# A sparse-attention and feed-forward kernel: sampled indices packed and loaded once, gathers and values' results for eight heads of a tile, and a schedule built from other durations

## The chip, the cores and the metric

The kernel runs on one core of a Trainium2 chip. The number that counts is the time of one execution in microseconds (us) on that core. A core has a matrix engine (TensorE, PE in the rows), three engines for elementwise work (VectorE or DVE, ScalarE or ACT, GpSimd or POOL), a queue engine that here only issues DMAs (SyncE or SP), and 16 DMA engines that serve the DMAs of all queues. Each engine runs its own instructions in order; an instruction that waits holds up all that stand behind it on that engine.

## The reference

Block-sparse attention over 4 batches, 8 heads, 768 positions and 64 channels, then a feed-forward layer. Each query block of 32 positions sees its neighbours, the first and last block, and three blocks that `sampled_blocks` names; the first and last query block see everything. The feed-forward weights are stored as float64.

```python
scores = scale * np.matmul(q, k.transpose(0, 1, 3, 2))
mask = np.abs(blk_i - blk_j) <= window
mask = mask | (blk_i == 0) | (blk_j == 0) | (blk_i == n_blocks - 1) | (blk_j == n_blocks - 1)
for qb in range(n_blocks):
    for kb in sampled_blocks[qb]:
        mask[qb * block:(qb + 1) * block, kb * block:(kb + 1) * block] = True
scores = np.where(mask, scores, -1000000000.0)
attn = np.exp(scores - np.max(scores, axis=-1, keepdims=True))
attn = attn / (np.sum(attn, axis=-1, keepdims=True) + 1e-09)
x = np.matmul(attn, v)            # (B, H, S, D), then to rows of H * D
h = x @ w_in                      # (3072, 512) @ (512, 2048)
g = np.maximum(h, 0.0) + alpha * np.minimum(h, 0.0)
out = g @ w_out                   # (3072, 2048) @ (2048, 512)
```

## The kernel before

Every number is split into a high and a low half in float16, and a product is the sum of high times high, high times low and low times high.

Attention is cut into 48 **units** (batch `b`, query tile `t` of 128 positions, half `c` of four heads). A tile is shifted by 32 positions, so that five of the six tiles of a batch hold only sparse blocks (40 sparse units), and the sixth holds the first and last block (8 dense units). A sparse unit goes through these steps:

- `emit_kr` (POOL): gathers the sampled blocks of the transposed keys into `kr`, 12 copies whose source address is a register. `picks` loads the 12 registers (L526) for each unit.
- `emit_vr` (SP): gathers the sampled blocks of the split values from a scratch tensor in DRAM into `vr`, 12 DMAs with an address from a register (L538), and again 12 register loads ahead of them on SP.
- `emit_s`, `emit_r` (PE): scores into the four PSUM banks `sp`.
- softmax: `emit_bias` (DVE, L635), `emit_exp` (ACT, L642), the two halves `ph` (`emit_p_hi`, `emit_p_lo`), and `emit_p_t` (SP, L683), a DMA transpose of `ph` to `pt`.
- `emit_r`, `emit_av` (PE, L555): values into one PSUM bank `av` per unit, `[hi part | low part]` beside each other, so that one matmul of 128 columns and one of 64 do a product.
- `evict`: the sum of the two parts (`emit_x_sum`, DVE, L688), the softmax division (L693), the split (L697, L701), and a DMA transpose on SP (L708) into `x`.

The feed-forward layer (`moe`) works on 12 chunks of 256 rows. A chunk has eight pairs of an up group `emit_up` (24 matmuls, L1050, into the one PSUM bank `h`) and a down group `emit_down` (12 matmuls, L1085). Between them stand `emit_act` on DVE (L1059, L1060), `emit_gh` on ACT and `emit_gl` on POOL (L1068). A chunk needs `x` of two tiles.

At the start, 16 pieces each of `w_in` (`wi`) and `w_out` (`wo`) are loaded, turned from float64 into float32 on DVE (L909, L916, L921), squared and scaled. The scale of `wo` is one for the whole matrix: a sum over all 16 pieces (`emit_o_tot`) and a matmul that spreads it (`emit_o_bc`, through L482).

What sets the order: each step is entered in a `Plan` with a priority, a cost in us for each engine that may do it, and buffers that it takes and frees. `Plan.run` plays the steps through and hands out an order, which is then fixed on every engine. The costs written there are a gather of values on SP at 1.5, a gather of keys on POOL at 5.0, a transpose on SP at 2.4, and loads on ACT alone at 0.06.

## Time and profile before

| | us |
|---|---|
| median of 3 runs | 1015.63 (1012.66 to 1015.92) |
| the profiled execution | 1017.7 |
| its span, first to last instruction | 1015.6 |
| PE busy in the span | 761.2 |
| mean granted clock of TensorE | 0.865 |

A row of the waits names the engine and the line that waited, what it waited for, the total in us, the number of waits and the longest. A row of the windows gives, for a stretch, its length and then the busy time of PE, PE's weight loads (PEld), DVE, ACT and POOL, the granted clock of TensorE, the share of the 16 DMA engines that was busy, and GB/s. "SPq" is SP issuing. A row of the timeline is a run of instructions with its start, its length, and in brackets the idle time ahead of it.

### The profile page before, as it was taken

To read this page: it belongs to the slowest core of one execution; us is meant where nothing else is said; L and a number is where in the kernel's file an instruction comes from. 1 tells how busy PE (TensorE), PEld (TensorE's weight loads), DVE (VectorE), ACT (ScalarE), POOL (GpSimd) and SP (SyncE) were. 2 spreads that over 40 slices of the span, in tenths; PEclk is the share of its full clock that TensorE was granted. 3 is DMA by queue.
4 is the path that set the end of the run, shared out by engine and by line. 5 is a ranking of instruction groups with operands and counts; after the bars stand their busy time and mean duration, and the time that the engine had idled before them with its cause. 6 is when DMAs were issued, how large, how long until landed. Compare 5 with 4: busy or idle time off the path is not lost.

```text
span 1015.6 us, 22541 instructions
## 1 busy us (share of the span) xinstructions
PE 761.2 (75%) x7931; PEld 510.4 (50%) x7931; DVE 638.9 (63%) x1535; ACT 374.7 (37%) x854; POOL 330.0 (32%) x676
## 2 busy tenths in 40 slices
...
GB/s 219 211 284 169 207 167 108 158 161 149 165 146 128 149 91 76 154 157 174 170 134 146 111 89 148 145 147 166 161 120 164 108 82 133 76 99 140 53 26 21
DMA packets 378737, 139.94 MB, mean 138 GB/s; under 512 B 338161, under 2 KB 367873, under 8 KB 378625
## 3 DMA queue, kind: packets, MB, share of 16 engines
...
## 4 chain that ended last, share of the span: by engine, by line
PE 32%; issue 13%; DMA 9%; DVE 8%; SPq 5%; POOL 3%; ACT 2%; POOLq 1%; ACTq 1%; DVEq 0%
PE h L1050 13%; PE o L1085 12%; PE sp L555 4%; DMA pt<-ph 3%; PE av L555 3%; SPq L538 2%; POOL gl L1068 2%; SPq L526 2%; DVE g L1059 2%; DVE ph L364 1%; POOL kr L550 1%; DMA qs<-qt 1%; DVE g L1060 1%; DMA x<-xn 1%; DMA qt<-qn 1%
## 5 line engine op out<-in xcount | busy, mean ns | idle before, releaser
L1050 PE MATMUL h<-x,wi 128*128 128x256 f16 x2304 | 286.0, 284 | 21.7 <-DVE g L1060 14.8
L1050 PEld LDWEIGHTS <-wi 128*128 128x128 f16 x2304 | 231.2, 102 | 67.4 <-issue 23.6
L1085 PE MATMUL o<-wo,gh 128*128 128x512 f16 x768 | 243.2, 400 | 1.5 <-ACT gh L1064 1.5
L1068 POOL TENSOR_TENSOR gl<-g,gh 128x512 f16<-128x512 f32 x96 | 117.6, 1226 | 371.7 <-ACT gh L1064 349.8
L550 POOL COPY kr<-kt 128x128 f16 x480 | 153.4, 374 | 179.2 <-PE sp L555 128.2
L1085 PE MATMUL o<-wo,gl 128*128 128x512 f16 x384 | 153.8, 401 | 25.4 <-POOL gl L1068 25.4
L1059 DVE TENSOR_SCALAR g<-h,am 128x256 f32<-128x256 f32 x192 | 83.8, 478 | 139.2 <-PE h L1050 132.8
L1064 ACT CAST gh<-g 128x512 f16<-128x512 f32 x96 | 59.1, 615 | 293.1 <-DVE g L1060 267.9
L642 ACT ACTIVATE e<-e,nm 128x352 f32<-128x352 f32 x160 | 92.6, 579 | 79.3 <-DVE nm L635 47.0
L364 DVE SCALAR_TENSOR_TENSOR ph<-e,ph 128x704 f16<-128x704 f32 (+1 forms) x106 | 102.7, 976 | 25.2 <-ACT ph L356 25.0
L1085 PEld LDWEIGHTS <-gh 128*128 128x128 f16 x768 | 73.8, 102 | 82.5 <-issue 16.2
L555 PEld LDWEIGHTS <-pt 96*32 96x32 f16 (+1 forms) x2304 | 74.0, 106 | 77.3 <-DMA pt<-ph 58.6
L555 PE MATMUL sp<-kt,qt 128*128 128x192 f16 (+2 forms) x384 | 67.1, 257 | 55.7 <-DVE nm L635 40.1
L635 DVE CUSTOM_DVE_ANT_0 e<-sp,bias,cs 128x352 f32<-128x352 f32 x160 | 86.8, 575 | 20.8 <-PE sp L555 20.7
L555 PE MATMUL sp<-kt,qs 128*128 128x192 f16 (+2 forms) x384 | 67.7, 259 | 16.3 <-DMA qs<-qt 16.3
L1085 PEld LDWEIGHTS <-gl 128*128 128x128 f16 x384 | 39.3, 102 | 80.3 <-POOL gl L1068 31.6
L555 PEld LDWEIGHTS <-qt 128*32 128x32 f16 (+1 forms) x1024 | 46.7, 104 | 62.7 <-issue 34.8
L1060 DVE SCALAR_TENSOR_TENSOR g<-h,gsc,g 128x512 f32<-128x512 f32 x96 | 72.1, 751 | 3.4
L555 PE MATMUL av<-vr,pt 96*32 96x128 f16 (+1 forms) x1280 | 28.9, 233 | 50.3 <-DMA pt<-ph 49.4
L555 PEld LDWEIGHTS <-qs 128*32 128x32 f16 (+1 forms) x1024 | 45.3, 104 | 38.8 <-issue 19.7
L356 ACT ACTIVATE ph<-e 128x704 f16<-128x704 f32 (+1 forms) x62 | 49.7, 804 | 32.6 <-DMA pt<-ph 17.9
L688 DVE TENSOR_REDUCE xf<-av 128x256 f32<-128x512 f32 x48 | 32.8, 684 | 44.3 <-PE av L555 44.3
...
## 6 DMA issues: line engine op xcount, KB each, us to landing
...
```

What stands on the lines that cost most here:

```text
L356: nc.scalar.activation(dst, src, AF.Copy, scale=scale)
L364: nc.vector.scalar_tensor_tensor(dst, src, scale, hi, ALU.mult, ALU.subtract)
L550: nc.gpsimd.tensor_copy(kr[:, :, g, r * BLK : (r + 1) * BLK], kt[:, :, bass.ds(i * BLK, BLK)])
L555: nc.tensor.matmul(dst, lhs, rhs, start=start, stop=False, skip_group_check=True)
L635: nc.vector.tensor_tensor_reduce(T["e", u, h // 2][:, h % 2, :CS], T["sp", u, h][:, :CS], bias[:, t], scale=T["cs", b, t][:, c : c + 1], s ...
L642: nc.scalar.activation(e, e, AF.Exp, bias=T["nm", u, h], scale=-1.0, accum_out=su_of(u)[:, h : h + 1])
L1050: nc.tensor.matmul(ph[:, i, :], win(w, f, ct), x[:, ct // 2, l, ct % 2, :], start=(m == 0), stop=(m == len(terms) - 1))
L1059: nc.vector.tensor_scalar(g[:, i, :], ph[:, i, :], 0.0, am1[:, f : f + 1], ALU.min, ALU.mult)
L1060: nc.vector.scalar_tensor_tensor(g, ph, gsc[:, j : j + 1], g, ALU.mult, ALU.add)
L1064: nc.scalar.copy(T["gh", c, j], T["g", c, j])
L1068: nc.gpsimd.tensor_tensor(T["gl", c, j], T["g", c, j], T["gh", c, j], ALU.subtract)
L1085: nc.tensor.matmul(T["o", c][t], g[:, i, t * P : (t + 1) * P], wout(w, f), start=(f == 0 and m == 0), stop=(f == NF - 1 and m == 2),)
```

## The change

Five things are different.

- **Indices.** Two block numbers are packed into one word (`spack`, DVE), and POOL and SP each load 30 registers once, at the program's start. A gather takes its 12 numbers from them by a mask or a shift. The loads of 12 registers, 40 on SP and 40 on POOL, are gone.
- **Gathers of values.** `emit_vr` runs once for a tile and fetches all eight heads: 20 times 12 DMAs of 64 KB instead of 40 times 12 of 32 KB.
- **Values' results.** The eight heads of a tile share one PSUM bank. A product takes three matmuls of 64 columns that add into the same place, where it took one of 128 and one of 64; the sum over the two parts falls away, and division, split and transpose run once for a tile (24 times instead of 48). The scale of `v` is found for each half of the heads, and the division evens the two out (`fac`).
- **Start.** Keys of the first batch and the first query tile are transposed by PE (with copies on ACT or DVE) and no longer by DMA. Loads may be issued by SP as well as ACT. In batches after the first, the small matmuls for the scales of `k` and `v` go to the bank `h`, which the up groups use, instead of `av`.
- **Schedule.** Costs and priorities in the plan are others, and steps of one kind are chained in order. `P_PE = 0` leaves all transposes of `ph` with SP.

```diff
-MOE_LAG = 7.669
+MOE_LAG = 14.222
 MOE_BOOST = 7.439
-V_WI = -2.266
+V_WI = 2.0
 W_WI = 0.799
-V_WO = -2.974
+V_WO = 4.06
...
-PL_V = -35.527
-P_V = 3.0
-LD = 5
+PL_W = 30.0
...
+P_V = -3.693
+P_K0, P_K1 = -10.0, 3.746
+KB0, KB1, KL0, KL1 = -5.461, -8.133, -22.947, -14.0
+VB0, VB1, VL0, VL1 = -4.453, -6.0, -20.0, -9.725
+GK, GV = (6, 3), (5, 3)
+P_Q, PL_Q = 10.31, 12.632
+A_UP = 0.511
+X_UP = 0.863
+LD = 3
 LAG = 0
 RAWP = ["x", "vr"]
-BUFS = {"vf": 4, "qf": 1, "qn": 1, "qt": 2, "qs": 2, "ph": 4, "e": 3, "pt": 5, "xf": 1, "xn": 2, "x": 3,
-        "g": 3, "sid": 1, "kt": 3, "v2": 3, "vb": 2, "vr": 2, "kr": 2, "gh": 3, "gl": 3}
+KVP = ["vf", "x"]
+BUFS = {"vf": 3, "qf": 1, "qn": 1, "qt": 2, "qs": 2, "ph": 4, "e": 3, "pt": 4, "xf": 1, "xn": 1, "x": 3,
+        "g": 3, "sid": 1, "kt": 3, "v2": 5, "vb": 2, "vr": 2, "kr": 2, "gh": 3, "gl": 3}
+K_PE = 2
...
     sidx = cpool.tile([1, NBLK, NR], I32, name="sidx")
+    spack = cpool.tile([1, TS * NG4 * NR // 2], I32, name="spack")
...
+    pairs = sidx.rearrange("p a r -> p (a r)")[:, NR : NR + TS * NG4 * NR].rearrange("p (n w) -> p n w", w=2)
+    nc.vector.scalar_tensor_tensor(
+        spack, pairs[:, :, 1], 16, pairs[:, :, 0], ALU.logical_shift_left, ALU.bitwise_or
+    )
+    idx = {}
+    for name, eng in (("g", nc.gpsimd), ("s", nc.sync)):
+        regs = [eng.alloc_register(name=f"{name}{i}") for i in range(TS * NG4 * NR // 2)]
+        eng.load(regs, spack)
+        idx[eng] = []
+        for r in regs:
+            v = eng.snap(r)
+            idx[eng] += [
+                nc.s_assert_within(x, 0, NBLK - 1, skip_runtime_bounds_check_because="clamped to this range before the load")
+                for x in (v & 0xFFFF, v >> 16)
+            ]
...
-    LQ = {"ACT": 0.06}
-    MAX4 = {"DVE": (0.55, 0), "ACT": 0.85, "POOL": 1.05}
-    LOW4 = {"DVE": (0.94, 0), "POOL": (1.05, 1.65)}
-    PHI = {"DVE": (0.55, 0), "ACT": 0.85}
+    LQ = {"ACT": 0.45, "SP": 0.35}
+    LQ3 = {"ACT": 1.3, "SP": 1.0}
...
+    def emit_k_pe(b, c, h):
+        if ("kt", b, c) not in T:
+            T["kt", b, c] = wt("kt", [P, HQ, S], F16)
+        nat = kn_view(b, c, h // 2)
+        t = T["kp", b, c, h] = ps_o.tile([P, 2 * DM], F16, tag="o", name="kp")
+        for i in range(NT):
+            g = (h % 2) * NT + i
+            nc.tensor.transpose(t[:, i * P : (i + 1) * P], nat[:, g].rearrange("p a d -> p (a d)"), ident16)
...
-    def picks(eng, name, t, use):
-        regs = [eng.alloc_register(name=f"{name}{i}") for i in range(NG4 * NR)]
-        eng.load(regs, sidx[0:1, 4 * t + 1 : 4 * t + 1 + NG4].rearrange("p a r -> p (a r)"))
-        for i, reg in enumerate(regs):
-            use(i // NR, i % NR, eng.snap(reg, min_val=0, max_val=NBLK - 1))
-        for reg in regs:
-            eng.free_register(reg)
-
-    def emit_vr(u):
-        b, t, c = units[u]
-        T["vr", u] = vr = wt("vr", [KR, NG4, HQ, P], F16)
+    def picks(eng, t, use):
+        for i in range(NG4 * NR):
+            use(i // NR, i % NR, idx[eng][NG4 * NR * t + i])
+
+    def emit_vr(b, t):
+        T["vr", b, t] = vr = wt("vr", [KR, NG4, H, P], F16)
         scr = T["scr", b]
 
         def use(g, r, i):
-            nc.sync.dma_start(
-                vr[r * BLK : (r + 1) * BLK, g], scr[bass.ds(i * BLK, BLK), c * HQ : (c + 1) * HQ, :]
-            )
-
-        picks(nc.sync, f"v{u}_", t, use)
+            nc.sync.dma_start(vr[r * BLK : (r + 1) * BLK, g], scr[bass.ds(i * BLK, BLK)])
+
+        picks(nc.sync, t, use)
...
-    def new_av(u):
-        T["av", u] = ps_a.tile([P, 512], F32, tag="av", name="av")
-
-    def av_view(u):
-        return T["av", u].rearrange("p (h a d) -> p h a d", h=HQ, a=2)
+    def av_of(u):
+        b, t, c = units[u]
+        if c == 0:
+            T["av", b, t] = ps_a.tile([P, H, D], F32, tag="av", name="av")
+        return T["av", b, t]
...
-            new_av(uv)
-            av = av_view(uv)
+            b, t, c = units[uv]
+            av = av_of(uv)
             for h in range(HQ):
                 pt = T["pt", uv, h // 2]
-                for x in range(2):
+                for x, y in TERMS:
                     for g in range(NG4):
                         r = slice(g * BLK, (g + 1) * BLK)
-                        lhs = pt[:KR, (h % 2) * 6 + 3 * x + 2, r]
-                        rhs = T["vr", uv][:, g, h, :]
-                        if x == 0:
-                            mm(av[r, h].rearrange("p a d -> p (a d)"), lhs, rhs, h == 0)
-                        else:
-                            mm(av[r, h, 0], lhs, rhs[:, :D], False)
-
-    def av_mm(u, h, pt, x, i, v, start):
-        av = av_view(u)
-        mm(av[:, h].rearrange("p a d -> p (a d)"), pt[:, 6 * x + i, :], v, start)
-        mm(av[:, h, 0], pt[:, 6 * x + 3 + i, :], v[:, :D], False)
+                        lhs = pt[:KR, PT(h % 2, x, 2), r]
+                        rhs = T["vr", b, t][:, g, c * HQ + h, y * D : (y + 1) * D]
+                        mm(av[r, c * HQ + h], lhs, rhs, (c, h, x, y) == (0, 0, 0, 0))
+
+    TERMS = ((0, 0), (0, 1), (1, 0))
+
+    def PT(a, x, i):
+        return (2 * a + x) * 3 + i
+
+    def av_mm(dst, pt, a, i, v, start):
+        for x, y in TERMS:
+            mm(dst, pt[:, PT(a, x, i), :], v[:, y * D : (y + 1) * D], start and (x, y) == (0, 0))
+
+    def v_tile(b, c, t, h):
+        return T["v2", b, c, t // 3][:, t % 3, h, :]
...
-    def emit_x_sum(u):
-        T["xf", u] = wt("xf", [P, HQ, D], F32)
-        av = T["av", u].rearrange("p (h a d) -> p h d a", h=HQ, a=2)
-        nc.vector.tensor_reduce(T["xf", u], av, AX.X, ALU.add)
-
-    def emit_x_mul(e, u):
+    def emit_x_mul(b, t):
+        T["xf", b, t] = wt("xf", [P, H, D], F32)
+        nc.vector.tensor_tensor(
+            T["xf", b, t], T["av", b, t], T["rs", b, t].unsqueeze(2).broadcast_to([P, H, D]), ALU.mult
+        )
...
-            T["x", cc][:, 4 * c : 4 * c + 4, (t % 2) * P : (t % 2 + 1) * P], T["xn", u].rearrange("p a c -> p (a c)")
+            T["x", cc][:, :, (t % 2) * P : (t % 2 + 1) * P], T["xn", b, t].rearrange("p a c -> p (a c)")
...
+        ab = plan.buf("o" if b == 0 else "h")
+        o = plan.op(prio - 4, {"PE": 0.6}, lambda: emit_v_bc(b, c), [o], [ab])
+        o_sv[b, c] = plan.op(prio - 4, {"DVE": 0.5}, lambda: emit_v_scale(b, c), [o], [], [ab])
...
+            T["ovr", b, t] = plan.op(n - 3, {"SP": 6.3}, lambda: emit_vr(b, t), o_scr[b] + gate + chain("vr"), [T["vrb", b, t]], dma=2.0)
+            tail["vr"] = T["ovr", b, t]
             vbb[b, t] = plan.buf("vb")
-            o_vb[b, t] = plan.op(n - 3, LQ, lambda e: emit_vb(e, b, t), o_scr[b] + gate_v, [vbb[b, t]], dma=0.9)
-
-    def evict(u, o, ab):
-        b, t, c = units[u]
+            o_vb[b, t] = plan.op(n - 3, LQ3, lambda e: emit_vb(e, b, t), o_scr[b] + gate, [vbb[b, t]], dma=0.6)
...
-        o = plan.op(p - 2, {"DVE": 0.78}, lambda: emit_x_sum(u), [o], [fb], [ab])
-        o = plan.op(p - 2, {"DVE": (0.4, 0), "POOL": (0, 0.65)}, lambda e: emit_x_mul(e, u), [o, T["ors", u]], [], [fb])
-        o = plan.op(p - 2, {"ACT": 0.42}, lambda: emit_x_hi(u), [o], [nb], [fb])
-        o = plan.op(p - 2, {"DVE": (0.4, 0), "POOL": (0, 0.65)}, lambda e: emit_x_lo(e, u), [o], [], [fb, nb])
-        o_x[u] = plan.op(p - 2, {"SP": 0.9}, lambda: emit_x_t(u), [o], [xbuf[cc]], [nb], dma=0.8)
+        ors = plan.op(p + 2, {"DVE": 0.25}, lambda: emit_rs(b, t), [e for c in range(NQ) for e in T["ex", uid[b, t, c]]] + [o_fac[b]])
+        o = plan.op(p - X_UP, {"DVE": 0.78}, lambda: emit_x_mul(b, t), [o, ors], [fb], [ab])
+        o = plan.op(p - X_UP, {"ACT": 0.62}, lambda: emit_x_hi(b, t), [o], [nb], [fb])
+        o = plan.op(p - X_UP, {"DVE": (0.74, 0), "POOL": (0, 1.2)}, lambda e: emit_x_lo(e, b, t), [o], [], [fb, nb])
+        o_x[b, t] = plan.op(p - X_UP, {"SP": 1.6}, lambda: emit_x_t(b, t), [o], [xbuf[cc]], [nb], dma=1.5)
...
             use += T["sbs", us] + [T["krb", us], qtbuf[b, t], qsbuf[b, t]]
-            cost += 0.55
+            cost += 0.35
...
             b, t, c = units[uv]
-            T["ab", uv] = ab = plan.buf("a")
-            deps += [T["ovr", uv]] + T["opt", uv]
-            alloc.append(ab)
-            use += [T["vrb", uv]] + T["ptb", uv]
-            cost += 0.6
+            if c == 0:
+                T["ab", b, t] = plan.buf("a")
+                alloc.append(T["ab", b, t])
+            else:
+                deps += [T["oav", uv - 1]]
+                use.append(T["ab", b, t])
+            deps += [T["ovr", b, t]] + T["opt", uv]
+            use += [T["vrb", b, t]] + T["ptb", uv]
+            cost += 0.4
...
-                o = plan.op(4 * u + h - 1, {"DVE": 0.58}, lambda h=h: emit_bias(u, h), [orand, o_cs[b, t, c], o_bias[t]] + ex[-1:], [eb],
+                o = plan.op(4 * u + h - A_UP, {"DVE": 0.61}, lambda h=h: emit_bias(u, h), [orand, o_cs[b, t, c], o_bias[t]] + ex[-1:], [eb],
                             [T["sbs", u][h]])
-                ex.append(plan.op(4 * u + h - 1, {"ACT": 0.56}, lambda h=h: emit_exp(u, h), [o], [], [eb]))
```

Three places show how the order moves. The first is SP around the second gather of values, before: `ph` are split probabilities, `qn` split queries, `sidx` the sampled indices, `scr` the values in DRAM.

```order
L683 DMA_TRANSPOSE pt<-ph_103 128x12x128
L683 DMA_TRANSPOSE pt<-ph_104 128x12x128
L683 DMA_TRANSPOSE pt<-ph_101 128x12x128
L426 DMA_TRANSPOSE qt<-qn 128x8x128
L526 TENSOR_LOAD sidx
L528 ISA
L538 DMA vr<-scr_457 32x512
```

After the change, SP around its first gather:

```order
L465 DMA_TRANSPOSE qt<-qn 128x8x128
L772 DMA_TRANSPOSE pt<-ph_101 128x12x128
L772 DMA_TRANSPOSE pt<-ph_102 128x12x128
L418 DMA wo<-in_moe_w_in_dram 128x4x256 x2
L772 DMA_TRANSPOSE pt<-ph_103 128x12x128
L623 REGISTER_ALU
L623 ISA
L623 DMA vr<-scr_594 32x1024
```

The register load is gone from this place, a DMA moves twice the columns, and loads of weights now stand between the transposes. A whole gather is 12 such DMAs in both.

The second place is PE at the matmul that spreads the sum of the squares of `wo` (`otot`), before. It stands behind the second unit's values, and no up group stands ahead of it.

```order
L555 LDWEIGHTS pt
L555 MATMUL av<-vb,pt 128x64
L482 MATMUL tot<-ident,otot 128x128
L555 LDWEIGHTS pt
L555 MATMUL av<-vr,pt 32x128
```

After the change:

```order
L638 LDWEIGHTS pt
L638 MATMUL av<-vr,pt 32x64
L565 MATMUL tot<-ident,otot 128x128
L638 LDWEIGHTS pt
L638 MATMUL av<-v_684,pt 128x64
```

It now stands behind five up groups (120 matmuls) and inside the sixth unit's values. The first up group itself has moved little: it stands behind the values of five units before, of four now.

The third place is the start, where ACT issued the first loads alone. Before, on ACT:

```order
L243 ACT_TABLE_LOAD
L243 ACTIVATE warm<-ones 128x1
L379 DMA kf<-in_k_dram 128x12x64 x2
L379 DMA qf<-in_q_dram 128x8x64
L379 DMA kf<-in_k_dram 128x12x64 x2
L379 DMA wo<-in_moe_w_in_dram 128x4x256 x5
```

After the change, on SP:

```order
L323 TENSOR_LOAD spack
L326 ISA x3
L418 DMA kf<-in_k_dram 128x12x64
L418 DMA qf<-in_q_dram 128x8x64
L418 DMA kf<-in_k_dram 128x12x64
L418 DMA vf<-in_v_dram 128x4x64 x3
```

Half of the first keys and the first queries are issued by SP, behind its load of the 30 registers, which needs `spack`. ACT still issues two pieces of keys, one of values and one of weights (1.7 MB together) ahead of its first instruction that needs a piece of SP's.

More of the change, by code (lines that the diff above doesn't have):

```diff
@@ L78, in op, with fits @@
         return o
+    def fits(self, bufs):
+        free = dict(self.free)
+        for b in bufs:
+            if not b.live:
+                pool = next((x for x in b.pools if free[x] > 0), None)
+                if pool is None:
+                    return False
+                free[pool] -= 1
+        return True
     def run(self):
@@ L134, in run @@
                 for o in ready:
-                    if any(not b.live and all(self.free[x] <= 0 for x in b.pools) for b in o.alloc):
+                    if not self.fits(o.alloc):
                         continue
@@ L369, in attn_moe @@
     T = {}
-    LQ = {"ACT": 0.06}
-    MAX4 = {"DVE": (0.55, 0), "ACT": 0.85, "POOL": 1.05}
-    LOW4 = {"DVE": (0.94, 0), "POOL": (1.05, 1.65)}
-    PHI = {"DVE": (0.55, 0), "ACT": 0.85}
+    LQ = {"ACT": 0.45, "SP": 0.35}
+    LQ3 = {"ACT": 1.3, "SP": 1.0}
+    MAX4 = {"DVE": (0.57, 0), "ACT": 0.89, "POOL": 1.05}
+    LOW4 = {"DVE": (1.0, 0), "POOL": (1.0, 1.65)}
+    PHI = {"DVE": (0.55, 0), "ACT": 0.8}
     kbuf, vbuf, qtbuf, qsbuf, xbuf, vbb = {}, {}, {}, {}, {}, {}
-    o_s, o_kt, o_v2, o_qt, o_qs, o_cs, o_pt, o_x, o_sv, o_scr, o_vb, o_rk, o_first = ({} for _ in range(13))
+    o_s, o_kt, o_v2, o_qt, o_qs, o_cs, o_pt, o_x, o_sv, o_scr, o_vb, o_rk, o_first, o_fac = ({} for _ in range(14))
     def load(e, dst, src):
@@ L724, in prep_k @@
         kbuf[b, c] = plan.buf("kt")
-        o_kt[b, c] = []
+        o_kt[b, c], los = [], []
         for i in range(2):
@@ new lines, in prep_k @@
+            los.append((o, nb))
+            if b == 0 and c < K_PE:
+                continue
+            o_kt[b, c].append(plan.op(prio - 2, {"SP": 1.8}, lambda i=i: emit_k_t(b, c, i), [o], [kbuf[b, c]], [nb], dma=2.3))
+        for h in range(HQ if b == 0 and c < K_PE else 0):
+            tb = plan.buf("o")
+            o, nb = los[h // 2]
+            o = plan.op(prio - 2, {"PE": 0.4}, lambda h=h: emit_k_pe(b, c, h), [o], [tb, kbuf[b, c]], [nb])
+            o_kt[b, c].append(plan.op(prio - 2, {"ACT": 0.85, "DVE": 0.9}, lambda e, h=h: emit_k_copy(e, b, c, h), [o], [kbuf[b, c]], [tb]))
@@ L771, in gather @@
-    def gather(u, gate_k, gate_v):
+        if (b, t) < (0, Q_PE):
+            for x, d, qb in ((0, o_qt, qtbuf[b, t]), (1, o_qs, qsbuf[b, t])):
+                tb = plan.buf("o")
+                o2 = plan.op(prio - 2, {"PE": 0.5 + 0.5 * x}, lambda x=x: emit_q_pe(b, t, x), [o], [tb, qb], [nb])
+                d[b, t] = plan.op(prio - 2, {"ACT": 1.1, "DVE": 1.2}, lambda e, x=x: emit_q_copy(e, b, t, x), [o2], [qb], [tb])
+            return
+        o_qt[b, t] = o = plan.op(prio - 2, {"SP": 1.45}, lambda: emit_q_t(b, t), [o], [qtbuf[b, t]], [nb], dma=1.55)
@@ L819, in random_part, with p_pt @@
+            use += [T["vrb", b, t]] + T["ptb", uv]
+            cost += 0.4
             p = max(p, 4 * uv + 4.5)
         return plan.op(p, {"PE": cost}, lambda: emit_r(us, uv), deps, alloc, use)
+    def p_pt(u, x, n, o, pb, ptb):
+        if 2 * u + x >= P_PE:
+            return [plan.op(n, {"SP": 1.55}, lambda: emit_p_t(u, x), [o], [ptb], [pb], dma=2.2)]
+        out = []
+        for z in range(2):
+            tb = plan.buf("o")
+            t = plan.op(n - 1, {"PE": 0.4}, lambda z=z: emit_p_pe(u, x, z), [o], [tb, ptb], [pb])
+            out.append(plan.op(n - 1, {"ACT": 0.85, "DVE": 0.9}, lambda e, z=z: emit_p_copy(e, u, x, z), [t], [ptb], [tb]))
+        return out
@@ L1112, in moe @@
         if ci == 0:
-            o_fs[b] = plan.op(start - 3, {"DVE": 0.5}, lambda: emit_fs(b), [o_sv[b], o_gsc, o_swo])
+            o_fs[b] = plan.op(start - 3, {"DVE": 0.5}, lambda: emit_fs(b), [o_fac[b], o_gsc, o_swo])
         obufs = [plan.buf("o") for _ in range(2)]
@@ L1116, in moe @@
         downs = []
-        xs = [o_x[uid[b, t, q_]] for t in (2 * ci, 2 * ci + 1) for q_ in range(NQ)]
+        xs = [o_x[b, t] for t in (2 * ci, 2 * ci + 1)]
         last = None
```

308 lines of the change are left out of this document (176 added, 132 removed).

## The prediction

> **What bounds the kernel now.** I read the windows first, cut where the stages change: loads alone, weights and first units, a hole, the way to the first up group (183.5 us), the middle, and the last chunk.
>
> ```profile
> core 0: us, PE busy (x) PEld busy (x) DVE busy (x) ACT busy (x) POOL busy (x), PEclk, DMA share, GB/s
> 0.00:25.00 25.00, 2.60 (x9) 2.18 (x9) 9.29 (x34) 10.88 (x21) 9.77 (x45) 1.00 0.98 218
> 25.00:120.00 95.00, 49.21 (x365) 27.05 (x366) 69.81 (x175) 50.28 (x121) 38.05 (x85) 0.71 0.89 215
> 120.00:143.00 23.00, 3.05 (x59) 2.54 (x56) 19.90 (x42) 7.59 (x20) 0.00 (x0) 0.57 0.81 229
> 143.00:183.50 40.50, 13.88 (x257) 11.08 (x256) 28.89 (x67) 15.65 (x36) 15.00 (x37) 0.54 0.55 118
> 183.50:966.00 782.50, 649.91 (x6965) 439.67 (x6963) 498.04 (x1197) 282.98 (x645) 257.95 (x501) 0.90 0.69 132
> 966.00:1015.60 49.60, 42.59 (x290) 27.84 (x287) 13.01 (x24) 7.33 (x12) 9.23 (x8) 0.99 0.06 22
> ```
>
> Three stages: 183.5 us of start, in which DMA and then DVE are the fullest; 782.5 us in which PE is busy for 649.9 and idle for 132.6; and 49.6 us of a last chunk with PE nearly full. In the middle PE also runs at a granted clock of 0.90, so about 650 x 0.10 = 65 us of its busy time are lost to the clock. The waits of PE in that window say what the 132 us are:
>
> ```profile
> PE av L555 <- DMA pt<-ph: 51.0, 19, 8.9
> PE o L1085 <- POOL gl L1068: 24.8, 10, 6.2
> PE sp L555 <- DMA qs<-qt: 16.3, 3, 7.3
> PE sp L555 <- DVE nm L649: 15.2, 10, 3.2
> PE h L1050 <- DVE g L1060: 12.9, 7, 5.5
> PE h L1050 <- DMA x<-xn: 6.5, 2, 3.6
> PE sp L555 <- DVE nm L635: 2.9, 2, 2.2
> ...
> PE av L555 <- DVE xf L688: 0.9, 1, 0.9
> ```
>
> Transposes and swaps that SP issues end 51.0 + 16.3 + 6.5 = 73.8 us, POOL 24.8, DVE's scores and gates 31.0. So I looked at what SP does. Its register loads (durations as least, median, most) and a stretch of its timeline:
>
> ```profile
> L526 POOLq TENSOR_LOAD <-sidx x40: 2705/2716/7542, 39.9 to 862.3; - x40
> L526 SPq TENSOR_LOAD <-sidx x40: 2469/3074/4513, 80.5 to 896.5; - x40
> ```
>
> ```profile
> 574.21 7.09 SPq L538 DMA_DIRECT2D vr<-scr  x12
> 581.41 1.47 SPq L683 DMA_TRANSPOSE pt<-ph  x1
> 582.92 1.63 SPq L426 DMA_TRANSPOSE qt<-qn  x1
> 584.65 1.22 SPq L708 DMA_TRANSPOSE x<-xn  x1
> 585.98 1.29 SPq L683 DMA_TRANSPOSE pt<-ph  x1
> 591.10 6.94 SPq L538 DMA_DIRECT2D vr<-scr  x12
> 598.10 1.13 SPq L379 DMA_DIRECT2D qs<-qt  x2
> 599.33 1.24 SPq L708 DMA_TRANSPOSE x<-xn  x1
> ```
>
> A pair of sparse units costs SP 2 x 3.07 + 7.09 + 6.94 + 4 x 1.4 (`pt`) + 1.63 + 1.22 + 1.24 + 1.13 = 31 us. Before the first up group PE has done five units' values; 43 units in 782.5 us make 36 us for a pair. SP is about 85% full, in order, and a transpose behind a gather waits up to 10 us.
>
> **The change, part by part.** *SP in the middle.* For a pair, one gather remains (7.09: 12 DMAs of twice the bytes; the issue is the same), no load, four `pt`, one `x` of double width (between 1.24 and 2.48; I take 1.5): 7.09 + 5.6 + 1.63 + 1.5 + 1.13 = 17 us, 45% less. Loads that move to SP from ACT add to it; I have no row for them on SP; ACT issues two in 1.22 us (first row of the start of the queues, below), and at that SP stays under 20 us. Of the 73.8 us of waits between none and all go. I take two thirds, **-49**, since a queue at half its load holds up little and what remains is the softmax ahead of the transpose.
>
> *POOL.* The load (2.72) goes; the 12 copies stay:
>
> ```profile
> 595.07 3.13 POOL L550 COPY kr<-kt 128x128 f16 x12 [2.37 <-PE sp L555]
> ```
>
> So of the block in front of `gl` 2.72 of 5.85 us go, and I take half of the 24.8 us: **-12** (0 to -25).
>
> *Clock.* 65 us are lost beside 132 idle, 0.49 for each idle microsecond. 61 less idle give **-30** (0 to -65).
>
> *Values.* Three matmuls of 64 columns replace one of 128 and one of 64: 512 more over the whole array, 640 more on 32 rows of it. The timeline at full clock:
>
> ```profile
> 913.18 0.52 PE L555 MATMUL av<-vr,pt 96*32 96x128 f16 x32
> 913.64 2.79 PE L1050 MATMUL h<-x,wi 128*128 128x256 f16 x24
> 916.27 0.25 PE L555 MATMUL av<-v,pt 128*128 128x128 f16 x2
> 916.35 0.25 PE L555 MATMUL av<-vb,pt 128*128 128x128 f16 x2
> ```
>
> 32 small ones start within 0.46 us (14 ns each), and a pair of 128 and 64 columns starts 0.08 us after the last. The columns stay 192. So a third matmul costs between 0 and half a pair, 43 ns: 0 to 22 us, and the small ones 640 x 14 ns = 9 us at most. I take a third of the sum, **+10**. The Trainium skill (TensorE: Matmul & The Clock Gate, Back-to-back issue gap) gives about 81 ns for each weight load with its matmul of 128 columns; the rows here start two in 85 ns, so they do not agree, and by the page the 1152 would cost 93 us, an estimate.
>
> *Evictions on DVE.*
>
> ```profile
> L688 DVE TENSOR_REDUCE xf<-av 128x256 f32<-128x512 f32 x48 | 32.8, 684 | 44.3 <-PE av L555 44.3
> L693 DVE TENSOR_TENSOR xf<-xf,rs 128x256 f32<-128x256 f32 x40 | 19.5, 487 | 0.4
> L701 DVE TENSOR_TENSOR xn<-xf,xn 128x256 f16<-128x256 f32 x37 | 17.9, 484 | 12.6 <-ACT xn L697 11.5 <-DMA vr<-scr 1.1
> L1060 DVE SCALAR_TENSOR_TENSOR g<-h,gsc,g 128x512 f32<-128x512 f32 x96 | 72.1, 751 | 3.4
> ```
>
> 70 us go; 24 products and at most 24 splits at about 751 ns (L1060, the nearest row from PSUM with 512 columns) come, 36 us. The 34 us lie beside PE, which waits 0.9 us for this step today; I book 0. The small matmuls for scales move to bank `h`: 12 round trips over DVE, between 0 and the 5.5 us that PE waited longest there. With down groups and scores between them I book 0, inside the range.
>
> *Start.* The waits of PE between 100 and 183.5, and the start of the queues:
>
> ```profile
> PE sp L555 <- DVE nm L635: 27.4, 9, 9.6
> PE tot L482 <- DVE otot L947: 19.9, 1, 19.9
> ```
>
> ```profile
> 1.03 1.22 ACTq L379 DMA_DIRECT2D kf<-in_k_dram  x2
> ...
> 11.65 0.47 POOL L292 TENSOR_SCALAR sidx<-rawp 1x72 int32<-1x72 int32 x1 [3.17 <-DMA rawp<-in_sampled_blocks_dram]
> ```
>
> The 19.9 us behind `otot` held two finished units. In the new order five up groups (2.63 us each by the row at 913.64) and an attention unit stand ahead of it, 18 us of PE work that fills the hole. The preparation of `wo` on DVE does not shrink, so the first down group comes no earlier. Against it: SP's first load of keys waits for `sidx` (12.1) and 30 registers at 3.07 / 12 us each, 7.7 us, until 20; ACT's own 1.7 MB last 8 us at 218 GB/s. That is some 11 us without transfers in a stretch with a DMA share of 0.98; since DVE is the fuller one from 100 on, I book 2. The sum of the start is **-16** (-41 to +11). The Trainium skill (Runtime: NRT & Kernel Launch, Instruction fetch mechanics) gives about 200 ns for each register also in bulk, which would make the load 6 us; the row says 256 ns and decides.
>
> *End.* The last chunk needs its own `x` and keeps its 16 groups: 0.
>
> **The sum** is -49 - 12 - 30 + 10 - 16 = -97: a span of 1015.6 - 97 = 918.6. The profiled execution took 1017.7, 2.1 more than its span and 2.1 more than the median of 1015.63, so the same difference taken from the median is 918.5.
>
> **Rivals.** *The DMA engines hold the transposes, not SP.* For it: where PE waited 3.3 and 4.6 us for `pt`, the engines were full.
>
> ```profile
> 610.00:620.00 10.00, 3.55 (x44) 1.59 (x28) 5.38 (x14) 2.92 (x9) 4.01 (x13) 0.74 0.95 178
> ```
>
> Against it: the mean share in the middle is 0.69. The 73.8 us stay, and -12 - 6 + 10 - 16 = -24 remain: **992**, 15%.
>
> *The new order fits nearly everywhere.* Three quarters of the idle time go (-99), the clock gives -49, values +10, the start -30: **848**, 16%. For it: the order before counts 1.5 us for a gather that took SP 10. Against it: 31 us of waits for DVE have no part in that.
>
> *The one value bank, slower.* `av` is now held over both halves of a tile, and the next tile's values wait until one product on DVE has freed it. There are 23 such hand-overs. From 4.4 us each (101 / 23) the gain is gone; at 5.5, the longest wait for DVE in the middle, they cost 126: **1044**, 8%. Against it: 0.9 us over 48 hand-overs now, and up and down groups stand between.
>
> *Every added matmul pays its own weight load, slower.*
>
> ```profile
> L555 PEld LDWEIGHTS <-pt 128*128 128x128 f16 x1024 | 54.2, 103 | 12.0 <-DMA pt<-ph 4.1 <-issue 0.3
> ```
>
> If loads of 103 ns were not covered, 1152 of them would be 119 us: 918 - 10 + 119 = **1027**, 4%. Against it: two loads at 103 do not fit the 85 ns of a pair. The skill's 81 ns, named above, would make it about 1001, an estimate.
>
> **How the numbers follow.** The forecast has 57%, with a range of its own of 880 to 955. The range of 850 to 1000 takes in it, the first rival and half of the second, 80%. A measurement of this kernel can tell about 0.3% from no change. Faster: 57 + 15 + 16 = 88%; of the slower cases I put 2% within 0.3%, and 10% above it.
>
> **What would show it.** Right: no register loads on SP but one, PE's waits for `pt`, `qs` and `x` below 30 us, for `gl` near 12, a clock of 0.94 or more in the middle, and a first down group near 197. Wrong: waits for `pt` as long as now with SP idle (first rival), waits of `av` for DVE's product (third), triples of matmuls that start more than 120 ns apart (fourth), or a DMA share that falls to nothing between 10 and 20 us and moves all that follows by more than 2.

## The result and the profile after

The changed kernel took 853.84 us (median of 4 runs, 850.29 to 855.29), the kernel before 1015.77 us in the same comparison (1012.66 to 1018.97): a ratio of 0.84, with a 95% interval of 0.8363 to 0.8438. The profiled execution took 850.29 us with a span of 848.5 us; its mean granted clock is 0.935, where it was 0.865.

The windows of the changed kernel, cut at its first up group and at the first up group of the last chunk (columns as before):

```profile
0.00:153.50 153.50, 70.34 (x789) 45.35 (x789) 105.43 (x266) 75.30 (x181) 72.25 (x156) 0.74 0.89 203
153.50:798.80 645.30, 609.01 (x8075) 428.31 (x8076) 491.60 (x1155) 299.09 (x654) 270.53 (x505) 0.98 0.86 164
798.80:848.50 49.70, 44.70 (x301) 29.05 (x299) 13.02 (x24) 7.47 (x13) 10.39 (x9) 0.99 0.06 22
```

The start is 30 us shorter (183.5 before), the middle 137 us (782.6, from 183.5 to 966.1), the end is what it was. In the middle PE is idle for 36.3 us where it was 132.6, and its busy time fell from 650.0 to 609.0, at a granted clock of 0.98 (0.90 before). What PE waits for in that window (what it waited for, total, times, longest):

```profile
PE h L1174 <- DVE g L1184: 13.6, 13, 4.1
PE o L1209 <- ACT gh L1188: 6.1, 3, 3.2
PE o L1209 <- POOL gl L1192: 5.6, 5, 3.4
PE sp L638 <- DVE nm L722: 5.4, 4, 2.5
PE av L638 <- DMA pt<-ph: 2.9, 2, 2.4
PE sp L638 <- DVE nm L736: 1.1, 2, 0.7
PE h L1174 <- DVE vtot L570: 1.0, 1, 1.0
...
PE h L1174 <- DMA x<-xn: 0.2, 1, 0.2
```

The three waits for SP's DMAs, 73.8 us together before, are 3.1 us. The wait for `gl` went from 24.8 to 5.6. The waits for DVE fell from 31.0 to 21.1. No wait of `av` for DVE's product stands here, and none of `qs`.

The lines of the register loads (least, median, most; first and last start), of the first up and down groups and of `otot`:

```profile
L323 SPq TENSOR_LOAD <-spack x1: 2276/2276/2276, 11.0 to 11.0; - x1
L323 POOLq TENSOR_LOAD <-spack x1: 2463/2463/2463, 11.0 to 11.0; - x1
...
L1174 PE MATMUL h<-x,wi x2304: 269/273/421, 153.5 to 837.7; 128*128 128x256 f16 x192
...
L1209 PE MATMUL o<-wo,gh x768: 378/379/634, 183.6 to 843.5; 128*128 128x512 f16 x192
...
L1071 DVE TENSOR_REDUCE otot<-osum x1: 164/164/164, 176.2 to 176.2; 128x1 f32<-128x16 f32 x1
```

The single load of 30 registers took 2.28 us, less than the median of a load of 12 before (3.07). The first down group starts 7.4 us after `otot`.

### The profile page after: what moved, and what is told of

Its sections match the earlier page's. It is cut to its first block, busy times and chain, and to the rows that moved or that the text cites. A ratio compares the mean times of both kernels' runs of the same rounds, so it can differ in the third digit from the quotient of the medians.

```text
span 848.5 us, 24338 instructions
## 1 busy us (share of the span) xinstructions
PE 724.1 (85%) x9163; PEld 502.7 (59%) x9163; DVE 610.0 (72%) x1444; ACT 381.9 (45%) x846; POOL 353.2 (42%) x670
## 4 chain that ended last, share of the span: by engine, by line
PE 56%; DVE 15%; DMA 12%; issue 7%; POOL 4%; ACT 3%; SPq 1%; POOLq 1%; ACTq 1%; DVEq 0%
PE o L1209 21%; PE h L1174 21%; PE sp L638 6%; PE av L638 5%; DMA pt<-ph 3%; DVE ph L402 3%; DVE g L1183 2%; DMA raw<-in_moe_w_out_dram 2%; DMA vr<-scr 1%; PE d L1101 1%; POOL kr L633 1%; POOL gl L1192 1%; DMA qf<-in_q_dram 1%; DVE e L722 1%; DVE wo L402 1%
## 5 line engine op out<-in xcount | busy, mean ns | idle before, releaser
L1174 PE MATMUL h<-x,wi 128*128 128x256 f16 x2304 | 270.8, 275 | 14.9 <-DVE g L1184 13.6
L1192 POOL TENSOR_TENSOR gl<-g,gh 128x512 f16<-128x512 f32 x96 | 120.8, 1259 | 318.4 <-ACT gh L1188 289.9
L1174 PEld LDWEIGHTS <-wi 128*128 128x128 f16 x2304 | 223.7, 99 | 49.8 <-issue 16.6
L1209 PE MATMUL o<-wo,gh 128*128 128x512 f16 x768 | 233.5, 386 | 6.1 <-ACT gh L1188 6.1
L633 POOL COPY kr<-kt 128x128 f16 x480 | 162.1, 388 | 61.0 <-PE sp L638 56.0
L1209 PE MATMUL o<-wo,gl 128*128 128x512 f16 x384 | 147.8, 385 | 6.2 <-POOL gl L1192 6.2
L1183 DVE TENSOR_SCALAR g<-h,am 128x256 f32<-128x256 f32 x192 | 83.7, 477 | 89.2 <-PE h L1174 78.2
L402 DVE SCALAR_TENSOR_TENSOR ph<-e,ph 128x704 f16<-128x704 f32 (+1 forms) x110 | 109.6, 1004 | 14.2 <-ACT ph L394 13.8
L729 ACT ACTIVATE e<-e,nm 128x352 f32<-128x352 f32 x160 | 92.6, 579 | 48.6 <-DVE nm L722 28.0
L394 ACT ACTIVATE ph<-e 128x704 f16<-128x704 f32 (+1 forms) x68 | 54.4, 803 | 3.1 <-DVE g L1183 1.8
L638 PE MATMUL av<-v,pt 128*128 128x64 f16 x1056 | 55.2, 195 | 0.0
L747 ACT ACTIVATE e<-e,nm 128x768 f32<-128x768 f32 x32 | 29.8, 933 | 37.1 <-DVE nm L743 29.5
```

The costliest lines, as they stand in the source:

```text
L394: nc.scalar.activation(dst, src, AF.Copy, scale=scale)
L402: nc.vector.scalar_tensor_tensor(dst, src, scale, hi, ALU.mult, ALU.subtract)
L633: nc.gpsimd.tensor_copy(kr[:, :, g, r * BLK : (r + 1) * BLK], kt[:, :, bass.ds(i * BLK, BLK)])
L638: nc.tensor.matmul(dst, lhs, rhs, start=start, stop=False, skip_group_check=True)
L729: nc.scalar.activation(e, e, AF.Exp, bias=T["nm", u, h], scale=-1.0, accum_out=su_of(u, h))
L1174: nc.tensor.matmul(ph[:, i, :], win(w, f, ct), x[:, l, ct, :], start=(m == 0), stop=(m == len(terms) - 1))
```

## The experiments

Two theories stood against each other. **A**, that of the prediction: SP's work was the cause, and time taken off SP comes back on PE. **B**, from the prediction's second rival: the order was the cause, since it was built with a gather at 1.5 us that took SP 10. Each variant computes the whole reference. The table gives the median, the ratio to the kernel before measured on the same chip, and of the profiled execution the middle: from the first up group to that of the last chunk, PE's idle time in it, and SP's issue time (the durations of SP's register, move and DMA-issuing rows that start in the window added up, waits on semaphores left out).

| | us | ratio (95%) | middle | PE idle | SP issues |
|---|---|---|---|---|---|
| before | 1015.77 | | 782.6 | 132.6 | 614 |
| before, indices loaded once | 947.0 | 0.9305 (0.9278 to 0.9332) | 717.1 | 89.2 | 532 |
| before, costs as measured | 1019.72 | 1.0045 (1.0009 to 1.0081) | 804.7 | 163.6 | 631 |
| before, values as 64 columns | 1009.46 | 0.9937 (0.9901 to 0.9972) | 775.4 | 127.4 | 624 |
| changed | 853.84 | 0.84 (0.8363 to 0.8438) | 645.3 | 36.3 | 451 |
| changed, loads put back | 875.45 | 0.859 (0.8542 to 0.8638) | 667.0 | 55.2 | 493 |
| changed, gathers in halves | 948.98 | 0.9332 (0.9281 to 0.9383) | 736.4 | 106.7 | 533 |
| changed, halves as steps | 924.7 | 0.9108 (0.9058 to 0.9157) | 694.6 | 71.0 | 506 |
| changed, loads and halves | 979.44 | 0.9594 (0.9548 to 0.964) | 768.7 | 132.6 | 573 |
| changed, costs of before | 884.8 | 0.8681 (0.8638 to 0.8724) | 677.0 | 63.5 | 431 |
| changed, priorities of before | 917.14 | 0.9043 (0.8993 to 0.9093) | 707.1 | 82.2 | 428 |
| changed, no transposes on PE | 863.17 | 0.85 (0.8454 to 0.8546) | 626.6 | 31.1 | 412 |
| changed, SP's load later | 859.21 | 0.8453 (0.8419 to 0.8486) | 652.5 | 38.5 | 447 |
| changed, indices first on SP | 852.71 | 0.8391 (0.8345 to 0.8437) | 649.1 | 38.9 | 445 |

### Less work on SP in the old order

The kernel before, with the packed indices of the change and nothing else; every other instruction keeps its place:

```diff
+    spack = cpool.tile([1, TS * NG4 * NR // 2], I32, name="spack")
...
-    def picks(eng, name, t, use):
-        regs = [eng.alloc_register(name=f"{name}{i}") for i in range(NG4 * NR)]
-        eng.load(regs, sidx[0:1, 4 * t + 1 : 4 * t + 1 + NG4].rearrange("p a r -> p (a r)"))
+    def picks(eng, t, use):
+        for i in range(NG4 * NR):
+            use(i // NR, i % NR, idx[eng][NG4 * NR * t + i])
```

> The kernel before with the indices packed and loaded once (30 registers on SP and on POOL), its order otherwise untouched. In the middle SP is spared 34 loads (107.6 us of its 614) and POOL 31 (111.4 us). Theory A (SP's work is the cause: each microsecond taken off SP comes back as less waiting for its transposes): the loads are 6.1 of the 14 us that the change takes off SP for a pair of units, so 44% of the predicted -49 on SP, all of the -12 on POOL and the clock with them, -17: about 965 us. Theory B (the order is the cause: it was built with a gather at 1.5 us and stays as it was): less than half of that, 990 to 1010 us, and PE's wait for pt stays above 35 us.

It took 947.0 us: 70 us less, more than theory A expected. The waits of PE in its middle:

```profile
PE av L567 <- DMA pt<-ph: 25.6, 15, 6.3
PE sp L567 <- DVE nm L661: 18.8, 10, 5.0
PE h L1062 <- DVE g L1072: 12.1, 10, 3.1
PE sp L567 <- DMA qs<-qt: 9.8, 2, 5.2
PE o L1097 <- POOL gl L1080: 8.0, 7, 3.2
```

The wait for `pt` is half of the 51.0 it was, that for `x` is 0.7 (6.5 before), that for `gl` a third of 24.8. SP issues for 82 us less, and the middle is 65.5 us shorter, in an order that knows nothing of it. Not all of this is SP's: the edit takes as many loads off POOL. The waits for SP's three DMAs fell by 37.7 us, that for POOL's `gl` by 16.8.

### The same work in a better informed order

```diff
-        T["okr", u] = plan.op(n - 4, {"POOL": 5.0}, ...
-        T["ovr", u] = plan.op(n - 3, {"SP": 1.5}, ...
+        T["okr", u] = plan.op(n - 4, {"POOL": 5.85}, ...
+        T["ovr", u] = plan.op(n - 3, {"SP": 10.1}, ...
```

and so with SP's transposes (1.75), swap (1.1), `x` (1.5) and ACT's loads (0.6).

> The kernel before with only the plan's numbers changed to what its own trace shows (gather of values with its load on SP 10.1 in place of 1.5, of keys on POOL 5.85 for 5.0, transposes 1.75 for 2.4, swap 1.1 for 0.12, x 1.5 for 0.9, a load on ACT 0.6 for 0.06); every instruction stays, only the order moves. Theory A: SP has as much to do as before, so no gain beyond 1.5%, 1000 to 1030 us. Theory B: the order puts gathers where no transpose waits behind them, and at least half of the 74 us of waits for SP's DMAs go, with the clock: 900 to 960 us.

It took 1019.72 us, 0.4% more than before. Its waits of PE in the middle:

```profile
PE h L1050 <- DMA x<-xn: 48.6, 9, 10.8
PE tot L445 <- ACT wi L352: 34.1, 8, 13.5
PE h L1050 <- DVE g L1060: 33.0, 21, 4.9
PE sp L555 <- DMA qs<-qt: 20.1, 6, 8.8
```

The wait for `pt` is 1.8 us, and 48.6 us for `x`, another transpose on SP, stand in its place: the three waits for SP's DMAs make 70.5 us, where they made 73.8. The wait for `gl` fell to 7.2 us, but 34.1 us behind ACT's `wi` are new. The first up group comes 25 us earlier (158.0), and the middle is 22 us longer. With SP as full as before, true costs mostly chose who waits. Theory B falls in this form.

### The changed kernel with the old costs and the old priorities

First the costs of before for SP's steps, POOL's gather and the issue of loads, with all else as changed:

```diff
-        T["okr", u] = plan.op(n - 4, {"POOL": 3.2}, ...
+        T["okr", u] = plan.op(n - 4, {"POOL": 5.0}, ...
-            T["ovr", b, t] = plan.op(n - 3, {"SP": 6.3}, ...
+            T["ovr", b, t] = plan.op(n - 3, {"SP": 1.5}, ...
-    LQ = {"ACT": 0.45, "SP": 0.35}
-    LQ3 = {"ACT": 1.3, "SP": 1.0}
+    LQ = {"ACT": 0.06, "SP": 0.06}
+    LQ3 = {"ACT": 0.06, "SP": 0.06}
```

> The changed kernel with the plan's numbers of before for SP's steps, POOL's gather and the issue of loads (1.5 for the gather that takes SP 6 to 7 us, transposes 2.4, swap 0.12, x 0.9, key gather 5.0, a load 0.06); priorities, chains and all instructions as changed. Theory A: SP's work is as small as in the changed kernel, so under 875 us. Theory B: PE's wait for pt comes back, 30 us or more, and the time is 900 us or more.

It took 884.8 us, 31 more than the changed kernel and between the two expectations, though SP issues for 20 us less. PE's waits in the middle:

```profile
PE sp L638 <- DVE nm L722: 29.2, 9, 9.8
PE h L1174 <- DVE g L1184: 17.0, 13, 3.3
PE h L1174 <- DVE uq L383: 5.0, 2, 4.7
...
PE av L638 <- DMA pt<-ph: 2.6, 2, 1.4
```

The wait for `pt` did not come back. What the order costs stands as waits for DVE's scores (5.4 before this edit). Then the priorities of before, with the costs, the chains and all instructions as changed:

```diff
-MOE_LAG = 14.222
+MOE_LAG = 7.669
-V_WI = 2.0
+V_WI = -2.266
-V_WO = 4.06
+V_WO = -2.974
-P_Q, PL_Q = 10.31, 12.632
-A_UP = 0.511
-X_UP = 0.863
+P_Q, PL_Q = 7.0, 14.0
+A_UP = 1.0
+X_UP = 2.0
```

and so with the leads of keys, values and weights.

> The changed kernel with the priorities of before (the lag of the feed-forward part 7.669, weights and values of the first batch, the lead of the keys' and queries' preparation, the lead of softmax and eviction, five buffers' worth of loads ahead), costs, chains and instructions as changed. If SP's relief alone carries the result, as in the prediction: under 870 us, since the priorities change no engine's work. If the priorities share in it: 880 to 920 us, with PE waiting for DVE, not for pt.

It took 917.14 us, 63 more:

```profile
PE h L1174 <- DVE g L1184: 29.1, 13, 8.6
PE sp L638 <- DVE nm L722: 21.4, 8, 6.2
PE sp L638 <- DVE nm L736: 8.8, 8, 3.5
PE av L638 <- DMA pt<-ph: 6.5, 4, 3.7
```

SP issues no more than in the changed kernel, and PE hardly waits for `pt`. These 63 us hang on the priorities, and the waits that grew are those for DVE. In the trace the up groups of successive chunks then start, at first, by turns about 78 and 50 us apart (152.9, 230.7, 279.9, 357.9, 408.7).

### SP's work put back into the new order

The register loads of before, ahead of each gather (20 on SP, 40 on POOL); the gathers issued as halves; and both:

```diff
-            nc.sync.dma_start(vr[r * BLK : (r + 1) * BLK, g], scr[bass.ds(i * BLK, BLK)])
+            for c in range(NQ):
+                hh = slice(c * HQ, (c + 1) * HQ)
+                nc.sync.dma_start(vr[r * BLK : (r + 1) * BLK, g, hh], scr[bass.ds(i * BLK, BLK), hh])
```

> The changed kernel with SP's work of before put back at unchanged order: 12 registers loaded ahead of each gather (20 loads on SP, 40 on POOL), and each gather of a tile issued as 24 DMAs of 32 KB in place of 12 of 64 KB. SP gets 20 x 3.1 + 240 x 0.45 = 170 us more, about 620 of the 636 us of the middle. Theory A: waits for pt, qs and x of 60 us or more come back with their clock, 940 us or more. Theory B (the order hides SP's work): under 890 us. In between, both count.

> The changed kernel with only the register loads put back (12 registers ahead of each gather: 20 loads on SP, 40 on POOL), gathers as changed. Loads and halves together cost 126 us over the changed kernel, for about 170 us more on SP and 109 us more on POOL. If SP's added time alone sets the loss, in proportion: 62/170 of 126, +46 us, about 900. If POOL's 109 us (the keys' gather stands ahead of gl and of the scores) carry a good part: more than +70, over 925. If a queue with room left takes small additions at no cost: under +25, below 880.

> The changed kernel with only the gathers in halves (24 DMAs of 32 KB for a tile in place of 12 of 64 KB; 108 us more on SP, nothing on POOL). In proportion to SP's time: 108/170 of 126, +80 us, about 934. If POOL carried a good part of the loss with both: under +50, below 905. If the two share one threshold (SP full), the sum of this loss and that with the loads alone is well below 126.

Both together took 979.44 us, 126 more than the changed kernel, as theory A had it (940 or more). The waits of PE in its middle:

```profile
PE av L629 <- DMA pt<-ph: 59.5, 15, 11.6
PE h L1165 <- DVE g L1175: 22.4, 14, 7.6
PE h L1165 <- DMA x<-xn: 18.1, 4, 6.1
...
PE sp L629 <- DMA qs<-qt: 9.1, 2, 8.8
```

The same three waits as before the change are back, 86.7 us. The loads alone cost only 22 us, the least of the three expectations:

```profile
PE o L1198 <- POOL gl L1181: 15.8, 6, 8.8
PE h L1163 <- DVE g L1173: 11.6, 14, 1.8
PE av L627 <- DMA pt<-ph: 9.3, 5, 3.4
```

Of this, 10 us are the wait for `gl`, whose engine POOL has the 40 loads again (5.6 to 15.8), and 6 us the wait for `pt`. The halves alone, which put work on SP and on no other engine, cost 95 us:

```profile
PE av L640 <- DMA pt<-ph: 51.0, 15, 10.3
PE h L1176 <- DVE g L1186: 14.2, 11, 5.3
PE h L1176 <- DMA x<-xn: 13.2, 4, 6.2
...
PE sp L640 <- DMA qs<-qt: 9.1, 2, 8.6
```

Halves might also have cost the DMA engines more. The two pages list the hardware queues (packets, MB, share of 16 engines' span); first the changed kernel:

```profile
q1 hardware_dynamic: 304416, 107.92, 67.1%
```

and with halves:

```profile
q1 hardware_dynamic: 315936, 107.93, 60.0%
```

0.671 x 848.5 and 0.600 x 946.2 both make 568 to 569 us. The DMA engines did the work of this queue in the same time; what grew is SP's issuing. A gather is 12 DMAs, and they cost SP the same for 32 KB as for 64: the median of the DMA issue is 316 ns in both kernels, besides the move and the register operation ahead of it.

By the table, 42 us of issues more on SP (loads) made the middle 22 us longer, 82 us (halves) 91, and 122 us (both) 123: between half of the added time and a little more than all of it. The two losses taken apart make 117 us, a little below the 126 of both; a common threshold would have put them well below. Nor can a threshold be read from the share of the middle in which SP issues: it is 70% in the changed kernel, 72% with halves, 74% with the loads, 75% with both and 78% in the kernel before, and halves cost far more than the loads.

Was it the block of 24 DMAs, 14 us in one piece that the plan took for 6.3? A variant with the halves as two steps, each placed and costed:

```diff
-            T["ovr", b, t] = plan.op(n - 3, {"SP": 6.3}, lambda: emit_vr(b, t), ...
+        T["ovr", b, t, c] = plan.op(n - 3, {"SP": 6.3}, lambda: emit_vr(b, t, c), ...
```

> The changed kernel with the values fetched in halves again (12 DMAs of 32 KB, twice for a tile), each half now a step of its own that the plan places and costs at 6.3 us, so that no block on SP is longer than in the changed kernel; SP's added time is the same 108 us as with 24 DMAs in one block (948.98 us). If SP's total sets the time: 930 us or more. If it was the block of 14 us ahead of the transposes, or a plan that took it for 6.3: under 890 us.

It took 924.7 us, between the two. The waits in its middle:

```profile
PE h L1177 <- DVE g L1187: 23.9, 15, 4.8
PE av L640 <- DMA vr<-scr: 19.8, 16, 2.4
PE sp L640 <- DVE nm L724: 7.3, 6, 2.2
```

So 24 of the 95 us go when the block is cut and the plan knows of it, and 71 remain. Of these, 25 lie in the start: the first up group comes at 178.4 us, where it was 153.5, and why was not tried. The middle is 49 us longer, for 55 us more of issues.

### What three matmuls of 64 columns cost

The kernel before, with each product of 128 columns issued as two of 64 into the same places; evictions and order stay:

```diff
-        mm(av[:, h].rearrange("p a d -> p (a d)"), pt[:, 6 * x + i, :], v, start)
+        mm(av[:, h, 0], pt[:, 6 * x + i, :], v[:, :D], start)
+        mm(av[:, h, 1], pt[:, 6 * x + i, :], v[:, D:], False)
```

> The kernel before with each product of values as two matmuls of 64 columns into the same two places, in place of one of 128 (1152 more matmuls and weight loads, 640 of them on 96 x 32); evictions, gathers and the order as before. By the prediction's term: +10 us (0 to +31), 1016 to 1047. If every added matmul pays a weight load of 103 ns that nothing covers: +119, over 1120. If PE's waits for SP absorb it: no change within 0.3%.

It took 1009.46 us, 0.6% less, and the interval of the ratio ends at 0.9972. The 1152 more matmuls cost nothing that shows: in the middle PE is busy for 648.0 us, where it was 650.0. Why it is a little faster was not tried. The timeline of the changed kernel at full clock (start, length, form, count) says the same:

```profile
606.76 0.69 PE L638 MATMUL av<-v,pt 128*128 128x64 f16 x18
607.29 0.28 PE L638 MATMUL sp<-kt,qt 128*128 128x192 f16 x2
```

18 of them start within 0.53 us, 29 ns each, so three take 88 ns where a pair of 128 and 64 columns took 85. The Trainium skill (TensorE: Matmul & The Clock Gate, Back-to-back issue gap) gives the 81 ns, from which the prediction estimated 93 us, for 128 columns. For 1 to 64 columns the Trainium skill has about 25 ns in the same section, and the 29 ns here lie near that.

### The start

Keys and queries of the first batch transposed by SP's DMAs again (`K_PE = 0`, `Q_PE = 0`):

> The changed kernel with keys of the first batch and the first queries transposed by DMA from SP again (K_PE = 0, Q_PE = 0). If these transposes by PE are what brought the first up group from 183.5 to 153.5 us: first up group at 165 or later and the time up by 10 us or more. If the order and the split loads did it: within 5 us of the changed kernel.

The time rose by 9.3 us, just short of the 10 that were expected. The first scores, in the changed kernel

```profile
L638 PE MATMUL sp<-kt,qt x38: 190/246/367, 33.6 to 115.1; 128*128 128x192 f16 x19, 128*128 128x64 f16 x19
```

start at 33.6 us, and in this variant at 63.2:

```profile
L638 PE MATMUL sp<-kt,qt x32: 190/246/368, 63.2 to 97.4; 128*128 128x192 f16 x16, 128*128 128x64 f16 x16
```

30 us of head start become 33 us at the first up group (187.0 against 153.5) and 14.8 at the last chunk's (813.6 against 798.8); the middle is shorter by the rest, since more of the work was done by then (7737 matmuls in it, 8075 in the changed kernel's).

SP's load of the 30 registers moved to its first gather, so that its loads of keys start at 0.7 us in place of 14.0:

> The changed kernel with SP's load of the 30 registers placed ahead of its first gather in place of ahead of its first loads of keys, so that those are issued from 1 us on in place of 14 us. If the transfers bound the start (DMA share 0.60 from 10 to 20 us in the changed kernel, 0.96 before): the first up group comes 5 to 10 us earlier and the time falls by as much. If DVE or ACT bound it after that: less than 3 us either way.

It took 859.21 us, neither the gain nor the standstill that were expected. It is 5 us slower, but the intervals of the two ratios overlap, so the loss is not certain. The windows of its first 30 us:

```profile
0.00:10.00 10.00, 0.00 (x0) 0.00 (x0) 0.17 (x1) 1.49 (x2) 6.08 (x16) 1.00 0.99 175
10.00:20.00 10.00, 0.25 (x1) 0.17 (x1) 0.35 (x2) 0.94 (x2) 1.87 (x13) 1.00 1.08 247
20.00:30.00 10.00, 1.01 (x4) 0.93 (x4) 4.95 (x19) 5.36 (x12) 3.16 (x21) 1.00 0.18 53
```

The transfers came earlier (share 1.08 from 10 to 20 us where it was 0.60). But POOL's load of the indices was issued at 8.6 us in place of 7.1, `sidx` was computed at 15.2 in place of 10.3, and DVE works for 0.5 us of the first 20. That POOL's small loads waited among SP's large ones is inferred, not shown. In the kernel before, where ACT alone issued the large loads and the share was 0.94 and 0.96 in these 20 us, `sidx` came at 11.7.

Indices and `alpha` loaded first by SP, in place of last by POOL:

> The changed kernel with the two small loads of sampled indices and alpha issued first on SP, in place of last on POOL (where rawp lands at 11.1 us and SP's first load of keys waits for it until 14.0). If the start hangs on the indices: rawp lands near 4 us, the first up group comes 4 us or more earlier, 845 to 850 us. If SP's loads then only push back the other small loads of POOL, as with the register load moved behind the first loads (859.21 us): 855 us or more.

`sidx` is computed at 6.9 us in place of 10.3, SP's loads start at 10.7 in place of 14.0, and the first up group comes at 154.5, where it was 153.5. 852.71 us lies between the two expectations and is no gain. None of the variants beats the changed kernel by more than its interval.

## Why the prediction was right and where it was wrong

The side was right, and the time lies in the stated range of 850 to 1000, near its lower end and outside the forecast's own range of 880 to 955. The main mechanism was right: SP's relief is worth most (947.0 with the loads of SP and POOL gone from the old order, 948.98 with nothing but the halves back on SP in the new). Its sizes were not: the forecast was 918.5, and 162 us were gained where it had 97. That the time still lies in the range is luck in part, since 853.84 is near the 848 of a rival that had 16%. Term by term, of the two profiled spans (1015.6 to 848.5, -167):

| term | predicted | measured | from |
|---|---|---|---|
| PE's waits for SP's DMAs | -49 | -70.7 | 73.8 to 3.1 |
| for `gl` | -12 | -19.2 | 24.8 to 5.6 |
| for DVE | 0 | -9.9 | 31.0 to 21.1 |
| other idle time | 0 | +3.5 | rest of 132.6 to 36.3; for `gh` 6.1, where it was 1.5 |
| clock, and values +10 | -20 | -41.0 | PE busy in the middle, 650.0 to 609.0 |
| start | -16 | -30.0 | first up group, 183.5 to 153.5 |
| end | 0 | +0.2 | 49.5 to 49.7 |

- **SP.** The step that failed is "I take two thirds, **-49**, since a queue at half its load holds up little and what remains is the softmax ahead of the transpose". SP is not at half its load: it issues for 451 of 645 us, 70%. It was at 78% before, not 85, and its issues fell by 163 us, 27%, not by 45. The pair of units was the wrong measure: of the units in the middle before, only 34 load registers and gather on SP, the 12 transposes of keys (24.7 us, then 27.6) are not in it, and 26.5 us of other DMAs came to SP from ACT. Yet almost all of the wait went, and nothing remained of the softmax: PE waits 2.9 us for `pt`, 2.6 with the old costs and 6.5 with the old priorities. With 532 us of issues in the old order it waits 25.6, with 533 in the new (halves) 51.0. So this wait follows SP's work, and that the order has a part in it is not shown.
- **The order.** It stood among the rivals at 16% and 848 us, priced at -99 of idle time, -49 for the clock, +10 and -30; the trace has -96, -41 with the values, and -30. This rival came closest. In the changed kernel the new costs are worth 31 us and the new priorities 63 us, both by waits for DVE, which the forecast had left at 0. The argument against it, that "31 us of waits for DVE have no part in that", was wrong: those waits are where the order shows. But the order alone, in the kernel before, gave nothing with true costs (1019.72). Neither the new priorities in the kernel before, nor the old costs and priorities together in the new structure, were tried.
- **The clock.** The direction was right: with 96 us less idle the clock in the middle rose from 0.90 to 0.98. The price of 0.49 for each idle microsecond is open. At a lost share of 0.02 in place of 0.10, 12 of 609 us are lost where 65 were, 0.55 for each. But with loads and halves back in the new order PE is idle for 132.6 us again, at a clock of 0.91, and its busy time is only 27 us longer (636.1), 0.28 for each. How much of the -41.0 is the clock's, and how much comes from the new form of the values and from one unit's values more in the stage (four stand ahead of the first up group, where five did), was not separated.
- **Values.** +10 was too much; the split shows no cost, and three matmuls take 88 ns, not over 120. The fourth rival (a load of 103 ns for each) is out by it.
- **POOL.** Half of 24.8 was too little; putting the loads back brings 10 us of it.
- **The start.** The step that failed is "The preparation of `wo` on DVE does not shrink, so the first down group comes no earlier". In the trace before, `otot` stands at 140.1 us:

```profile
L947 DVE TENSOR_REDUCE otot<-osum x1: 169/169/169, 140.1 to 140.1; 128x1 f32<-128x16 f32 x1
```

57 us ahead of the first down group (197.3). `wo` did not hold that group. It stands behind the first up group (183.5), which needs `x` of two tiles, and the fourth transpose of `x` was issued at 178.66 and landed 4.7 us later:

```profile
178.66 1.74 SPq L708 DMA_TRANSPOSE x<-xn  x1
```

The changed kernel does attention earlier (first scores at 33.6) and `wo` later (`otot` at 176.2), and its first down group comes at 183.6. The 7.7 us for 30 registers were 2.28: a load costs no more for 30 than for 12. By the about 200 ns for each register in the Trainium skill (Runtime: NRT & Kernel Launch, Instruction fetch mechanics) it would be 6 us, an estimate; the measurement decides. The gap in the transfers came, but smaller than described (share 0.60 from 10 to 20 us), and the variants that fill it gained nothing.
- **The other rivals.** The DMA engines hold no transposes: the share in the middle rose to 0.86 and the waits for transposes went. The one value bank: no wait of `av` for the product on DVE in the middle. (Its 101 / 23 should be 97 / 23, 4.2 us; nothing hangs on that.) The evictions merged for a tile were not tried by themselves.
